# Seven half products for the last four chunks of a squared-ReLU FFN behind a retention layer

## The chip, the core and the metric

One core of a Trainium2 chip runs the whole kernel in one launch. The metric is device time in microseconds (us). Three runs of the kernel before are shown: 203.85, 206.41 and 206.54 us, so the median is 206.41.

The engines are called as in the profile: PE multiplies matrices into the accumulator memory PSUM, DVE and ACT do elementwise work and read PSUM, POOL does elementwise work between buffers in SBUF, SP issues the transfers.

## What is computed

```python
for t in range(S):                       # retention: 4 batches, 8 heads of 64, S = 768
    state = gamma * state + einsum('bhd,bhe->bhde', k[:, :, t], v[:, :, t])
    y[:, :, t] = scale * einsum('bhd,bhde->bhe', q[:, :, t], state)
x = y.transpose(0, 2, 1, 3).reshape(3072, 512)
h = maximum(x @ w_in, 0)                 # first FFN product, 512 -> 2048
out = h * h @ w_out                      # second FFN product, 2048 -> 512
```

Inputs and output are float32; the matrix products read bf16.

## The kernel before, in words

The 3072 rows are 24 chunks of 128 (`C`). For each chunk the kernel loads q, k and v, casts them to bf16 (`ck`, `cq`, `cv`: names that the code gives its operations), transposes k and q (by PE early on, by a transposing transfer `X` later, L753 to L777), and makes a *visit* (`visit`, L828): PE computes scores and state sums of chunk n into the PSUM tensor `sc` and the outputs of chunk m into `yy`. `V22.23` is the visit that finishes chunk 22 and begins 23, `V23.` the one that finishes 23. DVE turns `sc` into the masked scores (`P`, L867) and the new state (`S`, L880), and `yy` into the FFN's input `xt` (`Y`, L889).

The first product (`ffn1`, L917 to L963) goes by blocks, mostly of two chunks. A block has 2048 hidden columns; each operation `F1.b.f` covers two groups of 128 of them with 8 matmuls of 128x256 (L936) into one of four rotating PSUM tensors `fps`. ACT takes the ReLU into a float32 buffer `r` (`R`, L943; there are two such buffers), and ACT (L950) or DVE (L952) squares it into `h` (`Q`). Blocks 11 and 12 are chunks 20 to 23.

The second product of chunks 4 to 23 (`products`, L992 to L1084) is already done with seven products in place of eight for each pair of chunks. DVE makes five sums of parts of `h` (`S1`, `S2`, `S5`, `S6`, `S7`, L1007), PE does seven products `M1` to `M7` of 8 matmuls of 128x256 each (L1032), and DVE and ACT combine them on the way out of PSUM (`e4`, `cc` on ACT, L1054 and L1060; `t1`, `u1`, `w`, `c` on DVE, L1050). SP stores the results.

Operations are declared with what they read and write, and a planner (`Plan`, L19) places all of them before anything is recorded: at each step it takes the operation that can start first by its own assumed durations, with priorities (`prio`, `RANK`, `LAGS`) as tie breaks, `HOME` fixing the engine where several could do the work. It also picks the `fps` tensor. The order it finds is the program's order on each engine. On PE the end of that order is: the visits to `V23.` with blocks 10 and 11 and the products of chunks 14 and 16 between them, then block 12 among the products of 16 to 20, and last `M5.22 M2.22 M7.22 M6.22`.

Of the kernel before, what the change touches and what calls it, by code (L numbers as in the profile page):

```python
# [18 lines left out]
class Plan:  # L19
# [21 lines left out]
    def add(self, name, eng, dur, reads=(), writes=(), fn=None, prio=0.0, lat=0.0, bank=None, after=(), count=0, slot=None, lock=()):  # L41
# [24 lines left out]
        return i

    def schedule(self, nbanks, max_open, nslots):
# [33 lines left out]
        while done < n:  # L102
            best = None
            for eng, cand in pool.items():
                ef = eng_free[eng]
# [22 lines left out]
            (t, _, _), i, eng = best
            o = ops[i]
            for e in o["eng"]:  # L130
                pool[e].discard(i)
# [34 lines left out]
            else:  # L166
                if eng == "PE":
# [21 lines left out]
                    if any(before < x <= issued for x in range(self.BLOCK0 - self.AHEAD, issued + 1, self.BLOCK)):  # L189
# [66 lines left out]
CAST = {"k": {"DVE": 0.43, "ACT": 0.63, "POOL": 0.64}, "q": {"DVE": 0.43, "ACT": 0.63, "POOL": 0.64}}
WCAST = {"DVE": 0.43, "ACT": 0.63, "POOL": 0.64}
EVAC = {"ACT": 0.6, "DVE": 0.62}
WPRIO = {"in": -2.0, "out": 2.0, "sum": 3.0}
# [3 lines left out]
SQUARE = {"DVE": 0.7, "ACT": 0.63}  # L263
WSUM = {"DVE": 0.69}
ASUM = {"DVE": 0.69}
LAGS = {
    16: 4.0, 4: 10.75, 6: 18.25, 10: 2.25, 20: 1.75, 14: 3.0, 8: 2.25, 18: 3.0, 12: 1.75, 22: 2.0,
}
RELU = {"ACT": 0.6}
# [4 lines left out]
PAIRS_A = {"S1": ((0, 0), (1, 1), ALU.add, None), "S5": ((0, 0), (0, 1), ALU.add, None),  # L274
           "S2": ((1, 0), (1, 1), ALU.add, None), "S6": ((1, 0), (0, 0), ALU.subtract, (1, 0)),
           "S7": ((0, 1), (1, 1), ALU.subtract, (0, 1))}
HOME = {
# [930 lines left out]
```

## Time and profile before

| | |
|---|---|
| runs of the kernel before | 203.85, 206.41, 206.54 us |
| span of the profiled execution | 202.7 us |
| time of the profiled execution with what lies around the span | not given on its own; the span lies 1.15 us below the lowest run, 3.7 below the median |
| PE busy | 192.8 us, 3032 matmuls |
| DVE, ACT, POOL busy | 150.0, 130.3, 31.3 us |
| granted PE clock | 1.00 throughout |

The page first gives each engine's busy time, then the span in 40 slices (a digit is tenths of the slice that the engine was busy), then the chain of work that ended last, then groups of equal instructions. A duration in the groups runs from an instruction's start to its modelled end; instructions of one engine overlap at their ends, so the distance between starts is shorter: 8 matmuls of 128x256 take 0.87 us one behind the other although one alone is shown with 264 to 273 ns, and DVE operations of 0.69 us follow each other every 0.61.

### The profile page before, as it was taken

What the parts mean: (1) busy time and instruction counts of PE and PEld (TensorE: products, weight loads), DVE (VectorE), ACT (ScalarE), POOL (GpSimd) and SP (SyncE); (2) the same over time, 40 slices, a digit from 0 to 9 for tenths busy, and PEclk for the clock granted to TensorE, in tenths of its full rate; (3) what the DMA queues carried; (4) which work ended last, traced back from release to release, by engine and by line L of the source; (5) the groups of instructions that cost most, each with busy time, mean ns of one, the idle gap of its engine ahead of it and who ended that gap; (6) DMA issues with size and microseconds to landing.
All of it is one profiled execution on the core that took longest, in us unless ns stands there. A gap on an engine that the chain in (4) does not pass through costs nothing.

```text
span 202.7 us, 7020 instructions
## 1 busy us (share of the span) xinstructions
PE 192.8 (95%) x3032; PEld 159.4 (79%) x3032; DVE 150.0 (74%) x283; ACT 130.3 (64%) x229; POOL 31.3 (15%) x56
## 2 busy tenths in 40 slices
PE   8886999899989999999999999999999999999992
PEld 6554887664577888888888888888888888888881
DVE  3486449569849988969898888878998784934762
ACT  8565888788871883787975485569375873835210
POOL 6541252220102101310211012203010000000000
PEclk9999999999999999999999999999999999999999
DMA  5999999999999999999999999999676100111313
GB/s 159 290 314 320 348 344 330 361 246 210 236 191 219 231 247 212 205 234 186 148 240 165 261 211 218 178 222 194 143 145 97 48 17 3 52 52 55 102 55 105
DMA packets 97935, 38.46 MB, mean 190 GB/s; under 512 B 81008, under 2 KB 94320, under 8 KB 97904
## 3 DMA queue, kind: packets, MB, share of 16 engines
q1 hardware_dynamic: 97760, 37.89, 86.2%
q8 instruction: 23, 0.38, 0.8%
q10 hardware_dynamic: 144, 0.13, 0.2%
q14 instruction: 8, 0.07, 0.1%
HBM read 27.26 MB, written 6.29 MB: 166 GB/s over the span
## 4 chain that ended last, share of the span: by engine, by line
PE 75%; DMA 15%; SPq 5%; POOL 1%; DVE 1%; issue 1%; ACT 0%; DVEq 0%
PE fps L936 33%; PE fps L1032 29%; DMA kn<-in_k_dram 8%; PE fps L1108 6%; DMA wst<-in_moe_w_in_dram 4%; DMA qkT<-kqs 3%; SPq L910 3%; PE yy L787 2%; SPq L537 2%; PE yy L802 1%; PE sc L813 1%; PE sc L824 1%; POOL w_in L522 1%; DVE wu L1050 1%; POOL h L522 0%
## 5 line engine op out<-in xcount | busy, mean ns | idle before, releaser
L936 PE MATMUL fps<-xt,w_in 128*128 128x256 bf16 (+1 forms) x832 | 94.0, 264 | 1.6 <-ACT w_in L518 1.2
L936 PEld LDWEIGHTS <-w_in 128*128 128x128 bf16 x832 | 74.8, 98 | 11.5 <-ACT w_in L518 2.0
L943 ACT ACTIVATE r<-fps 128x512 f32<-128x512 f32 x96 | 56.4, 592 | 34.6 <-PE fps L936 28.6
L950 ACT ACTIVATE h<-r 128x512 bf16<-128x512 f32 x63 | 39.1, 627 | 1.4
L1032 PE MATMUL fps<-wst,h 128*128 128x256 bf16 x320 | 39.4, 273 | 0.0
L1032 PEld LDWEIGHTS <-h 128*128 128x128 bf16 x320 | 31.0, 98 | 3.9
L952 DVE TENSOR_TENSOR h<-r 128x512 bf16<-128x512 f32 x33 | 22.8, 705 | 8.7 <-ACT r L943 8.6
L1032 PEld LDWEIGHTS <-wst 128*128 128x128 bf16 x240 | 23.3, 98 | 2.8
L1007 DVE TENSOR_TENSOR wst<-h 128x1024 bf16<-128x1024 bf16 x30 | 19.4, 685 | 2.9 <-ACT h L950 2.6
L1032 PE MATMUL fps<-w_out,wst 128*128 128x256 bf16 x160 | 20.3, 273 | 0.0
L728 DVE TENSOR_TENSOR vs<-vn,vf 128x512 bf16<-128x512 f32 x20 | 13.8, 691 | 6.3 <-DMA vn<-in_v_dram 6.3
L889 DVE TENSOR_TENSOR xt<-yy,yf 128x512 bf16<-128x512 f32 x20 | 13.7, 687 | 3.5 <-PE yy L802 3.4
L522 POOL CAST kqs<-kn 128x512 bf16<-128x512 f32 x12 | 8.0, 666 | 51.0 <-DMA kn<-in_k_dram 32.3
L1108 PE MATMUL fps<-w_out,h 128*128 128x512 bf16 x64 | 15.0, 379 | 0.7 <-DVE w_out L520 0.7
L1007 DVE TENSOR_TENSOR h<-h 128x1024 bf16<-128x1024 bf16 x20 | 14.0, 729 | 0.2
L880 DVE TENSOR_TENSOR state<-sc,state 128x256 bf16<-128x256 f32 x33 | 13.8, 418 | 0.5
L867 DVE TENSOR_TENSOR pt<-sc,cmask 128x512 bf16<-128x512 f32 x20 | 13.6, 681 | 0.0
L522 POOL CAST kqs<-qn 128x512 bf16<-128x512 f32 x11 | 6.9, 626 | 42.9 <-DMA qn<-in_q_dram 30.6
L1050 DVE TENSOR_TENSOR wu<-fps,wu 128x512 f32<-128x512 f32 (+1 forms) x16 | 9.1, 572 | 5.0 <-ACT osb L1060 2.8
L1108 PEld LDWEIGHTS <-h 128*128 128x128 bf16 x64 | 5.9, 98 | 6.8 <-issue 0.8
L1060 ACT ACTIVATE osb<-fps 128x512 f32<-128x512 f32 x10 | 5.9, 594 | 8.3 <-PE fps L1032 8.3
L1050 DVE TENSOR_TENSOR osb<-fps,osb 128x512 f32<-128x512 f32 (+1 forms) x15 | 9.0, 601 | 2.6 <-PE fps L1032 1.7
(85 smaller groups left out, 173.4 us busy)
## 6 DMA issues: line engine op xcount, KB each, us to landing
qn<-in_q_dram SPq DMA_DIRECT2D x20, 256.0 KB, 5.1
kn<-in_k_dram SPq DMA_DIRECT2D x20, 256.0 KB, 5.6
vn<-in_v_dram SPq DMA_DIRECT2D x20, 256.0 KB, 5.2
out_dram<-osb SPq DMA_DIRECT2D x19, 256.0 KB, 3.3
wst<-in_moe_w_out_dram SPq DMA_DIRECT2D x4, 1024.0 KB, 10.1
wst<-in_moe_w_in_dram SPq DMA_DIRECT2D x4, 512.0 KB, 8.4
wst<-in_moe_w_in_dram SPq DMA_DIRECT2D x2, 1024.0 KB, 8.3
kn<-in_k_dram SPq DMA_DIRECT2D x2, 512.0 KB, 4.3
```

Source lines behind the costliest of these rows:

```text
L522: nc.gpsimd.tensor_copy(o, t)
L728: lambda: nc.vector.tensor_tensor(out=o[:], in0=t.rearrange("s (h d) -> s h d", h=H), in1=vf[:, i, :, None].to_broadcast([P, H, D]), op=AL ...
L880: f = lambda cc=cc, j1=j1, j0=j0: nc.vector.tensor_tensor(out=sts[j1][:], in0=cc, in1=sts[j0][:], op=ALU.add)
L889: lambda: nc.vector.tensor_tensor(out=xt[:, :, u * C : u * C + C].rearrange("s p (g t) -> s g p t", g=2), in0=yy[:, :, 0:256].rearrange("s ...
L936: nc.tensor.matmul(ps[:, u * n : u * n + n], lhsT=w_in_bf[j][:, cb, c * P : (c + 1) * P], rhs=xt[:, cb, cols], start=(cb == 0), stop=(cb = ...
L943: nc.scalar.activation(o, t, AF.Relu)
L950: nc.scalar.activation(hv, rv, AF.Square)
L952: (nc.vector if on == "DVE" else nc.gpsimd).tensor_tensor(out=hv, in0=rv, in1=rv, op=ALU.mult)
L1007: lambda on, o=a[name], x=a[x], y=a[y], op=op: (nc.vector if on == "DVE" else nc.gpsimd).tensor_tensor(out=o, in0=x, in1=y, op=op), prio=c ...
L1032: nc.tensor.matmul(ps[:, 256 * half : 256 * half + 256], lhsT=a[left][:, f], rhs=right(f), start=(first and f == 0), stop=True, skip_group ...
L1050: return lambda ps: nc.vector.tensor_tensor(out=o, in0=ps[:, lo:hi], in1=y, op=op)
L1108: nc.tensor.matmul(ps[:, 0:w], lhsT=h2[:, fb, u * C : u * C + C], rhs=w_out_bf[j][:, c, ns], start=(fb == 0), stop=(fb == NFB - 1))
```

## The change

Blocks 11 and 12 become one block of four chunks (`BLOCKS` ends in 4), done by a new function `ffn1_four`. With the hidden columns in two halves, the model dimension in two halves and the four chunks in two pairs, its eight half products become seven, in the Winograd form. Each of four steps t handles two groups of 128 hidden columns in either half:

- `WI1` to `WI4`, twice each: sums of parts of `w_in`, 128x1024 bf16, written into the load buffers of chunks 20 to 22 after their casts. Five are on DVE, three (`WI4.1`, `WI3.0`, `WI4.0`) on POOL.
- `TX0` to `TX3`: sums of parts of `xt`, 128x512 bf16, on DVE.
- `G1.t` to `G7.t` on PE: 4 matmuls of 128x256 each. `G1`, `G6`, `G7`, `G4` go on accumulating in one PSUM tensor, `G2` stands in a second, `G5` and `G3` accumulate in a third. The first two are the halves of `sc` for t = 0 and 2 and of `yy` for t = 1 and 3, the third is an `fps`.
- between them the accumulators are read while the chain is still open: `kc11`, `kc12`, `kc22` copy one to float32 buffers (11 on ACT, 1 on DVE), `c11`, `c12`, `c22` on DVE add another to the copy (128x512 float32), and `Qc` squares with ReLU: one operation on DVE (5 of them), or a ReLU in place and a square on ACT (7). The fourth quarter is read from the chain's end as before: `R.t` on ACT, `Q.t` on ACT (3) or DVE (1).

```diff
-BLOCKS = [2, 2, 1, 1, 2, 2, 2, 2, 2, 2, 2, 2, 2]
+BLOCKS = [2, 2, 1, 1, 2, 2, 2, 2, 2, 2, 2, 4]
...
+    def ffn1_four(blk):
...
+        for j in range(2):
+            for y, a, b, op in (("1", (1, 0), (1, 1), ALU.add), ("2", "1", (0, 0), ALU.subtract),
+                                ("3", (0, 0), (1, 0), ALU.subtract), ("4", (0, 1), "2", ALU.subtract)):
...
+        for y, a, b, op in ((0, part(0, 1), part(0, 0), ALU.subtract), (1, part(1, 1), tx[0], ALU.subtract),
+                            (2, part(1, 1), part(0, 1), ALU.subtract), (3, part(1, 0), tx[1], ALU.subtract)):
...
+                    for u in range(2):
+                        for k in range(2):
+                            nc.tensor.matmul(ps[:, 256 * u : 256 * u + 256], lhsT=left[i](2 * t + u, k), rhs=right[i][:, k],
+                                             start=(first and u == 0 and k == 0), stop=True, skip_group_check=True)
...
+                    if on == "ACT":
+                        nc.scalar.activation(x, x, AF.Relu)
+                        nc.scalar.activation(o, x2, AF.Square)
+                    else:
+                        (nc.vector if on == "DVE" else nc.gpsimd).scalar_tensor_tensor(
+                            out=o, in0=x2, scalar=0.0, in1=x2, op0=ALU.max, op1=ALU.mult)
...
+            mult(2, "W", True)
+            mult(1, "U", True)
+            kept("c11", "U")
+            both("c11", "W", bkeys["W"])
+            squared("c11", 0, 0)
+            mult(6, "U", False)
+            kept("c12", "U")
+            o1["op"] = pl.ops[mult(5, "V", True)]
+            kept("c22", "V")
+            mult(7, "U", False)
+            both("c22", "U", bkeys["U"])
+            squared("c22", 1, 1)
+            mult(3, "V", False)
+            both("c12", "V", bkeys["V"], bank=("close", ("V", t)))
+            squared("c12", 0, 1)
+            mult(4, "U", False)
```

The priorities and `HOME` go, and `TURNS` writes the order of every engine out by name. SP's order is the same to the end. PE's is the same up to `M4.14`, DVE's up to the sums of chunk 16, ACT's up to `Q10.2`, POOL's to its end, where the three sums are added. In the rest of the program the sums `S1` to `S7` of `products` are renamed `H1` to `H7`. Three squares of block 10 move from DVE to ACT. The end of the new PE order:

```
M4.14 F1.10.8 F1.10.6 V20.21 F1.10.10 F1.10.4 M1.14 M5.14 M2.14 F1.10.12 V21.22 F1.10.14 M6.14 M3.16 M7.14
V22.23 M4.16 M1.16 G2.0 G1.0 V23. M5.16 M2.16 G2.1 G5.0 G1.1 G6.0 M6.16 G3.0 G7.0 G6.1 G5.1 M7.16 G7.1 G4.0
G5.2 G3.1 G4.1 G2.2 M3.18 G1.2 G2.3 G1.3 G5.3 M4.18 G6.2 M1.18 G6.3 G3.2 G7.2 G3.3 G7.3 M5.18 G4.2 G4.3
M2.18 M6.18 M3.20 M4.20 M7.18 M1.20 M5.20 M2.20 M3.22 M4.22 M6.20 M7.20 M1.22 M5.22 M2.22 M7.22 M6.22
```

The planner's assumed durations change too; they move which of the four `fps` an operation gets, and three of the 36 filling matmuls of the start.

More of the change, by code (lines that the diff above doesn't have):

```diff
@@ L34 @@
     HOP = 0.15
+    LATE = 55
+    TAIL = {"DVE": 0.08, "ACT": 0.11, "POOL": 0.055}
     def __init__(self):
@@ L39, in __init__, with add @@
         self.readers = {}
-    def add(self, name, eng, dur, reads=(), writes=(), fn=None, prio=0.0, lat=0.0, bank=None, after=(), count=0, slot=None, lock=()):
+    def add(self, name, eng, dur, reads=(), writes=(), fn=None, lat=0.0, bank=None, after=(), count=0, slot=None, lock=()):
         i = len(self.ops)
@@ L84, in schedule, with offer @@
                 pool.setdefault(e, set())
-                if left[o["i"]] == 0:
-                    pool[e].add(o["i"])
+        known = {o["name"]: o["i"] for o in ops}
+        turns = {e: [known[x] for x in TURNS[e].split()] for e in pool}
+        assert sorted(i for x in turns.values() for i in x) == list(range(n))
+        for e, x in turns.items():
+            for i in x:
+                ops[i]["eng"] = {e: ops[i]["eng"][e]}
+        at = dict.fromkeys(pool, 0)
+        def offer():
+            for e, x in turns.items():
+                if at[e] < len(x) and left[x[at[e]]] == 0:
+                    pool[e].add(x[at[e]])
+        offer()
         if "PE" in eng_free:
@@ L188, in schedule @@
                     history.append((issued, t + dur))
-                    if any(before < x <= issued for x in range(self.BLOCK0 - self.AHEAD, issued + 1, self.BLOCK)):
+                    if t < self.LATE and any(before < x <= issued for x in range(self.BLOCK0 - self.AHEAD, issued + 1, self.BLOCK)):
                         behind = [x for x in moves if x[0] > t + 0.4]
@@ L221, in schedule @@
                 same = list(ops[u]["eng"]) == [eng] and not move
-                ready_at[u] = max(ready_at[u], start[i] + dur if same else end[i] + self.HOP)
+                ready_at[u] = max(ready_at[u], (start[i] + dur if eng not in self.TAIL else end[i] + 0.01) if same else end[i] + self.HOP)
                 left[u] -= 1
-                if left[u] == 0:
-                    for e in ops[u]["eng"]:
-                        pool[e].add(u)
+            offer()
         self.start, self.end, self.on = start, end, [o["on"] for o in ops]
@@ L241 @@
 WARMING = 18.4
-PACE = 8
-LEAD = 2
 NPE = 6
@@ L248 @@
 WHALFD = (0.60, 1.47, 33, 0.6)
-CVT = {'DVE': 0.69, 'POOL': 1.07}
-TCAST = {'DVE': 0.43, 'ACT': 0.63, 'POOL': 0.64}
-TEVAC = {'ACT': 0.6, 'DVE': 0.62}
+CVT = {'DVE': 0.602, 'POOL': 1.003}
+TCAST = {'DVE': 0.338, 'ACT': 0.52, 'POOL': 0.558}
+TEVAC = {'ACT': 0.48, 'DVE': 0.5}
 NPAIR = 2
-F2LAG = 3.5
 F2WAIT = 4
 LAST = [256, 128, 128]
[L256 to L259, printed above, removed]
+CAST = {"k": {"DVE": 0.338, "ACT": 0.52, "POOL": 0.558}, "q": {"DVE": 0.338, "ACT": 0.52, "POOL": 0.558}}
+WCAST = {"DVE": 0.338, "ACT": 0.52, "POOL": 0.558}
+EVAC = {"ACT": 0.48, "DVE": 0.341}
 BOTH = ("DVE", "POOL")
[L263 to L269, printed above, removed]
+SQUARE = {"DVE": 0.602, "ACT": 0.52}
+WSUM = {"DVE": 0.602}
+ASUM = {"DVE": 0.602}
+RELU = {"ACT": 0.48}
+FUSED = ()
+KEPT = {"ACT": 0.48, "DVE": 0.602}
+SQUARE2 = {"DVE": 0.602, "ACT": 1.1}
+WSUM2 = {"DVE": 0.602, "POOL": 2.0}
 APART = (22,)
@@ L273 @@
            "T6": ((0, 0), (0, 1), ALU.add), "T7": ((1, 0), (1, 1), ALU.add)}
[L274 to L277, printed above, removed]
[36 rows of a table removed]
-}
-ROUND = []
-RANK = {
[22 rows of a table removed]
-}
-ORDER = (
-    "k0 q0 v0 q2 k2 v2 i0 i1 i2 q4 i3 i4 k4 i5 v4 o0 q5 o1 k5 o2 o3 q6 v5 k6 v6 q7 k7 v7"
-)
-def dma_order(nm):
-    names = {"i": "in", "o": "out"}
-    seq = [(names.get(t[0], t[0]), int(t[1:])) for t in ORDER.split()]
-    return seq + [(x, m) for m in range(nm) for x in "kqv" if (x, m) not in seq]
+PAIRS_A = {"H1": ((0, 0), (1, 1), ALU.add, None), "H5": ((0, 0), (0, 1), ALU.add, None),
+           "H2": ((1, 0), (1, 1), ALU.add, None), "H6": ((1, 0), (0, 0), ALU.subtract, (1, 0)),
+           "H7": ((0, 1), (1, 1), ALU.subtract, (0, 1))}
+TURNS = {
+    "POOL": (
[3 rows of a table added]
+    ),
+    "DVE": (
[15 rows of a table added]
+    ),
+    "ACT": (
[13 rows of a table added]
+    ),
[8 rows of a table added]
+    ),
[16 rows of a table added]
+    ),
+}
 @with_exitstack
@@ L681, in add_up @@
                     nc.vector.tensor_tensor(out=sts[j1][:], in0=cc, in1=sts[j0][:], op=ALU.add)
-            pl.add(f"S{m + c}", {"DVE": 0.42, "ACT": 0.45} if first else "DVE", 0.42, (f"gB{m + c}",) if first else (f"gB{m + c}", f"S{j0}"), (f"S{j1}",), add_up,
-                   prio=urgency(m) - 0.5, bank=("close", ("B", m + c)))
+            pl.add(f"S{m + c}", {"DVE": 0.341, "ACT": 0.28} if first else "DVE", 0.341, (f"gB{m + c}",) if first else (f"gB{m + c}", f"S{j0}"), (f"S{j1}",), add_up, bank=("close", ("B", m + c)))
         for b2 in range(2):
@@ L703, in out_fn @@
                                         in1=f, op=ALU.mult)
-            pl.add(f"Y{m}.{b2}", "DVE", 0.68, banks[b2] + (f"yf{b2}", f"yf{2 + b2}"),
-                   [f"xt{g % NXT}.{u + c}" for c in range(2)], out_fn, prio=urgency(m))
+            pl.add(f"Y{m}.{b2}", "DVE", 0.602, banks[b2] + (f"yf{b2}", f"yf{2 + b2}"),
+                   [f"xt{g % NXT}.{u + c}" for c in range(2)], out_fn)
     def prepare(m):
@@ L812, in scores, with sums @@
                     cs = slice(sub * L, sub * L + L)
-                    nc.tensor.matmul(sc[cs, a, j * L : j * L + L], lhsT=qkT[r, 0, j, cs], rhs=qkT[r, 1, j, cs],
-                                     start=(j == 0), stop=True, skip_group_check=True)
-    def sums(m):
+                    nc.tensor.matmul(sc[cs, a, 256 * x + j * L : 256 * x + j * L + L], lhsT=qkT[r, 0, j, cs], rhs=qkT[r, 1, j, cs],
+                                     start=(j == 0 and x == 0), stop=True, skip_group_check=True)
+    def sums(m, ps=None, first=False):
         ks, vs = bf["k"][m % NBF], bf["v"][m % NBF]
@@ L823, in sums @@
                 for a in range(2):
-                    nc.tensor.matmul(sc[L * a : L * a + L, sub, 256 + j * D : 256 + j * D + D],
-                                     lhsT=ks[r, j, a, :], rhs=vs[r, 4 * a + j, :],
-                                     start=False, stop=True, skip_group_check=True)
+                    o = sc[L * a : L * a + L, sub, 256 + j * D : 256 + j * D + D] if ps is None else ps[sub][L * a : L * a + L, j * D : j * D + D]
+                    nc.tensor.matmul(o, lhsT=ks[r, j, a, :], rhs=vs[r, 4 * a + j, :],
+                                     start=(first and j == 0), stop=True, skip_group_check=True)
     def visit(m, n, t=None):
@@ L858, in visit @@
             dur += 0.2
-        pl.add(f"V{'' if m is None else m}.{'' if n is None else n}", "PE", dur, reads, writes, fn,
-               prio=-300 + n if m is None else -300 + m if m < PACE else (m - LEAD) * 8, lat=0.25,
+        pl.add(f"V{'' if m is None else m}.{'' if n is None else n}", "PE", dur, reads, writes, fn, lat=0.25,
                count=32 * ((m is not None) + (n is not None) + (t is not None)) + 1)
@@ L881, in visit @@
                         out=sts[j1][:], in0=cc, in1=sts[j0][:], op=ALU.add)
-                pl.add(f"S{n}.{sub}", "DVE", 0.42, (f"sc{sub}",) if first else (f"sc{sub}", f"S{j0}"), (f"S{j1}",), f,
-                       prio=urgency(n))
+                pl.add(f"S{n}.{sub}", "DVE", 0.341, (f"sc{sub}",) if first else (f"sc{sub}", f"S{j0}"), (f"S{j1}",), f)
         if m is not None:
@@ L887, in visit @@
             xt = xts[g % NXT]
-            pl.add(f"Y{m}", "DVE", 0.68, ("yy0", "yy1") + tuple(f"yf{p}" for p in range(NJ)), (f"xt{g % NXT}.{u}",),
+            i0 = pl.add(f"Y{m}", "DVE", 0.602, ("yy0", "yy1") + tuple(f"yf{p}" for p in range(NJ)), (f"xt{g % NXT}.{u}",),
                    lambda: nc.vector.tensor_tensor(
@@ L891, in visit, with visit2, fn, f @@
                        in0=yy[:, :, 0:256].rearrange("s g (p t) -> s g p t", p=NJ),
-                       in1=yf[:, :, i * C : i * C + C].rearrange("s p (g t) -> s g p t", g=2), op=ALU.mult),
-                   prio=urgency(m))
+                       in1=yf[:, :, i * C : i * C + C].rearrange("s p (g t) -> s g p t", g=2), op=ALU.mult))
+            y_made.append(i0)
+    def visit2(ms, ns):
+        reads, writes = [], []
+        for m in ms:
+            reads += [f"bfv{m % NBF}", f"pt{m % 2}"] + qkeys(m) + [f"S{state(m, 0)}", f"S{state(m, 1)}"]
+        if ms:
+            writes += ["yy0", "yy1"]
+        for n in ns:
+            reads += [f"bfk{n % NBF}", f"bfv{n % NBF}"] + qkeys(n)
+        o1 = {}
+        if ns:
+            writes += ["sc0", "sc1", f"gB{ns[0]}.0", f"gB{ns[0]}.1"]
+        def fn():
+            for x, m in enumerate(ms):
+                values(m, x)
+                apply(m, 0, x)
+            if ms:
+                nc.tensor.drain(fusable=True).then_inc(turn, 1)
+                turns[0] += 1
+            for x, n in enumerate(ns):
+                scores(n, x)
+            for x, n in enumerate(ns):
+                sums(n, [fps[o1[sub]["bank_index"]][:, 256 * x : 256 * x + 256] for sub in range(2)], x == 0)
+            if ms:
+                nc.tensor.wait_ge(turn, turns[0])
+                for x, m in enumerate(ms):
+                    apply(m, 1, x)
+        name = ".".join("-".join(str(x) for x in y) for y in (ms, ns))
+        if ns:
+            i0 = pl.add(f"U{name}", "PE", 0.0, reads, writes, lambda: None,
+                        bank=("open", ("U", ns[0], 0), False))
+            o1[0] = pl.ops[i0]
+        i0 = pl.add(f"V{name}", "PE", 0.2 + 0.26 * (len(ms) + len(ns)) + (0.2 if not ns else 0), reads, writes, fn, lat=0.25, count=32 * (len(ms) + len(ns)) + 1,
+                    bank=("open", ("U", ns[0], 1), False) if ns else None)
+        if ns:
+            o1[1] = pl.ops[i0]
+        for x, n in enumerate(ns):
+            pt = pts[n % 2]
+            pl.add(f"P{n}", "DVE", 0.602, ("sc0", "sc1", "cmask"), (f"pt{n % 2}",),
+                   lambda pt=pt, x=x: nc.vector.tensor_tensor(
+                       out=pt[:], in0=sc[:, :, 256 * x : 256 * x + 256].rearrange("s g (p t) -> s g p t", p=NJ),
+                       in1=cmask[:, None, None, :].to_broadcast([P, 2, NJ, L]), op=ALU.mult))
+            for sub in range(2):
+                if sub == 1 and where(n)[1] == NCH - 1:
+                    continue
+                j0, j1 = state(n, sub), state(n, sub + 1)
+                first = where(n)[1] == 0 and sub == 0
+                def f(j0=j0, j1=j1, first=first, sub=sub, x=x):
+                    cc = fps[o1[sub]["bank_index"]][:, 256 * x : 256 * x + 256].rearrange("s (p t) -> s p t", p=NJ)
+                    if first:
+                        nc.vector.tensor_copy(sts[j1][:], cc)
+                    else:
+                        nc.vector.tensor_tensor(out=sts[j1][:], in0=cc, in1=sts[j0][:], op=ALU.add)
+                users = 1 + (sub == 0 or all(where(y)[1] != NCH - 1 for y in ns))
+                pl.add(f"S{n}.{sub}", "DVE", 0.341, [f"gB{ns[0]}.{sub}"] + ([] if first else [f"S{j0}"]), (f"S{j1}",), f, bank=("close", ("U", ns[0], sub), users))
+        for x, m in enumerate(ms):
+            g, u = divmod(m, 4)
+            i = where(m)[1]
+            xt = xts[g % NXT]
+            pl.add(f"Y{m}", "DVE", 0.602, ("yy0", "yy1") + tuple(f"yf{p}" for p in range(NJ)), (f"xt{g % NXT}.{u}",),
+                   lambda xt=xt, u=u, i=i, x=x: nc.vector.tensor_tensor(
+                       out=xt[:, :, u * C : u * C + C].rearrange("s p (g t) -> s g p t", g=2),
+                       in0=yy[:, :, 256 * x : 256 * x + 256].rearrange("s g (p t) -> s g p t", p=NJ),
+                       in1=yf[:, :, i * C : i * C + C].rearrange("s p (g t) -> s g p t", g=2), op=ALU.mult))
@@ L945, in relu, with relu_square @@
                     nc.vector.tensor_scalar_max(o, t, 0.0)
+            def relu_square(f0=f0, o1=o1):
+                t = fps[o1["op"]["bank_index"]][:].rearrange("p (u n) -> p u n", u=per)
+                nc.vector.scalar_tensor_tensor(out=h2[:, f0 : f0 + per, cols], in0=t, scalar=0.0, in1=t,
+                                               op0=ALU.max, op1=ALU.mult)
             def square(on, f0=f0, o1=o1):
@@ L952, in square @@
                     (nc.vector if on == "DVE" else nc.gpsimd).tensor_tensor(out=hv, in0=rv, in1=rv, op=ALU.mult)
-            i0 = pl.add(f"F1.{blk}.{f0}", "PE", per * NCB * (n * 0.4167 + 3) / 1e3, reads, (f"g{grp}",), mm,
-                        prio=blk0[blk] * 8 + 2 * f0 * nb / 4, lat=0.2, bank=("open", grp, False),
-                        count=per * NCB)
+            hk = [f"h{g % NH2}.{u0 + w}.{f0 + u}" for u in range(per) for w in range(nb)]
+            i0 = pl.add(f"F1.{blk}.{f0}", "PE", per * NCB * (n * 0.4167 + (3 if n > C else 10)) / 1e3, reads, (f"g{grp}",), mm, lat=0.2, bank=("open", grp, False),
+                        count=per * NCB, after=openers.get(g - NH2, ()))
@@ L957, in ffn1 @@
+            f1_of.setdefault(g, []).append(i0)
             o1["op"] = pl.ops[i0]
-            hk = [f"h{g % NH2}.{u0 + w}.{f0 + u}" for u in range(per) for w in range(nb)]
-            i0 = pl.add(f"R{blk}.{f0}", RELU, 0, (f"g{grp}",), (f"r{grp}",), relu,
-                        prio=blk0[blk] + f0 / 16 * nb, bank=("close", grp), slot=("open", grp))
+            if f"{blk}.{f0}" in FUSED:
+                pl.add(f"RQ{blk}.{f0}", "DVE", 0.602, (f"g{grp}",), hk, relu_square,
+                       bank=("close", grp), after=twin_users if g == NH2 - 1 else pt_users if g == 1 else ())
+                continue
@@ L1033, in mm @@
                                      start=(first and f == 0), stop=True, skip_group_check=True)
-            k = pl.add(f"M{i}.{c0}", "PE", 0.877, key[left] + reads, (f"gS{c0}{bank}",), mm,
-                       prio=(c0 + 1 + LAGS.get(c0, F2LAG)) * 8 + count[0] * 16 / 7, lat=0.2,
+            k = pl.add(f"M{i}.{c0}", "PE", 0.877, key[left] + reads, (f"gS{c0}{bank}",), mm, lat=0.2,
                        bank=(bank_use, ("s", c0, bank), True) if bank_use == "open" else (bank_use, ("s", c0, bank)), count=8)
@@ L1038, in product, with read @@
             if first:
+                both_open.append(k)
+                openers.setdefault(g, []).append(k)
+            if first:
                 op["op"] = pl.ops[k]
-        def read(name, eng, dur, bank, reads, writes, fn, close=False, prio=0.0):
+        def read(name, eng, dur, bank, reads, writes, fn, close=False):
             pl.add(f"{name}.{c0}", eng, dur, [f"gS{c0}{bank}"] + list(reads), writes,
-                   lambda: fn(fps[opened[bank]["op"]["bank_index"]]), prio=c0 + 1 + prio,
+                   lambda: fn(fps[opened[bank]["op"]["bank_index"]]),
                    bank=("close", ("s", c0, bank)) if close else ("use", ("s", c0, bank)))
@@ L1069, in products @@
             product(7, "B", 0, "use")
[L1070 removed]
+            read("c", "DVE", 0.602, "B", kwu, kwu, on_psum(wu[:], 0, 512, wu[:], ALU.subtract), close=True)
         if last:
@@ L1078, in products @@
                         out[rows(c0) + lo * C : rows(c0) + lo * C + C, col : col + 256], wu[:, 256 * lo : 256 * lo + 256])
-                pl.add(f"st{c0}.{lo}", "ACT" if lo == 0 else "SP", STORE, k, (), f, prio=-1)
+                pl.add(f"st{c0}.{lo}", "ACT" if lo == 0 else "SP", STORE, k, (), f)
             return
@@ L1121, in ffn2 @@
                        lambda q4=q4, slot=slot, ns=ns, at_end=at_end: (nc.scalar if at_end else nc.sync).dma_start(
-                           out[rows(q4) : rows(q4) + C, ns], osbs[slot][:, ns]),
-                       prio=-1)
-    dma_prio = {x: n for n, x in enumerate(dma_order(NM))}
-    urgency = lambda m: m - 3.0
+                           out[rows(q4) : rows(q4) + C, ns], osbs[slot][:, ns]))
     for kind in pieces:
@@ L1141 @@
         n = m + 1
-        for x in range(0 if m < 0 else m + AHEAD, min(NM, m + AHEAD + 1)):
+        if n > DOUBLE:
+            xs = range(prepared, min(NM, n + AHEAD) if n % 2 else prepared)
+        else:
+            xs = range(0 if m < 0 else m + AHEAD, min(NM, m + AHEAD + 1))
+        for x in xs:
             prepare(x)
             transpose(x)
+            prepared = x + 1
         t = m + 2 if NPE <= m + 2 < NTD else None
-        if n < 2 * NPAIR:
+        if n >= DOUBLE:
+            if n % 2 == 0:
+                visit2([x for x in (n - 2, n - 1) if n > DOUBLE or x == n - 1], [x for x in (n, n + 1) if x < NM])
+        elif n < 2 * NPAIR:
             if n % 2 == 0:
@@ L1155 @@
         while done < NB and blk0[done] + blocks[done] - 1 == m:
-            ffn1(done)
+            (ffn1_four if blocks[done] == 4 else ffn1)(done)
             while done2 < NM and done2 + 2 <= blk0[done] and blk0[done] - done2 >= F2WAIT:
```

247 lines of the change are left out of this document (148 added, 99 removed), and 113 rows, old and new, of tables (HOME, RANK, TURNS).

## The prediction

> **What bounds the kernel now.** I read the page first, then the stage that the change touches by its busy times, its chain of waits, its idle PE time, and last some rows that price the new operations.
>
> ```profile
> span 202.7 us, 7020 instructions
> ...
> PE 192.8 (95%) x3032; PEld 159.4 (79%) x3032; DVE 150.0 (74%) x283; ACT 130.3 (64%) x229; POOL 31.3 (15%) x56
> ...
> PE   8886999899989999999999999999999999999992
> ...
> PEclk9999999999999999999999999999999999999999
> ...
> L943 ACT ACTIVATE r<-fps 128x512 f32<-128x512 f32 x96 | 56.4, 592 | 34.6 <-PE fps L936 28.6
> L950 ACT ACTIVATE h<-r 128x512 bf16<-128x512 f32 x63 | 39.1, 627 | 1.4
> ...
> L1007 DVE TENSOR_TENSOR wst<-h 128x1024 bf16<-128x1024 bf16 x30 | 19.4, 685 | 2.9 <-ACT h L950 2.6
> ...
> L880 DVE TENSOR_TENSOR state<-sc,state 128x256 bf16<-128x256 f32 x33 | 13.8, 418 | 0.5
> ...
> L1060 ACT ACTIVATE osb<-fps 128x512 f32<-128x512 f32 x10 | 5.9, 594 | 8.3 <-PE fps L1032 8.3
> ```
>
> PE is at 9 from about a third of the span to the end, at the full clock. The busy times by stretch begin where the orders part (147.8 is `V20.21`, 160.7 `V22.23`):
>
> ```profile
> 147.80:160.70 12.90, 12.90 (x237) 11.27 (x236) 10.79 (x20) 8.66 (x16) 0.61 (x1) 1.00 0.48 82
> 160.70:166.70 6.00, 6.00 (x109) 5.22 (x108) 5.23 (x10) 4.88 (x8) 0.00 (x0) 1.00 0.14 46
> 166.70:175.20 8.50, 8.42 (x106) 7.46 (x105) 5.36 (x10) 4.56 (x9) 0.00 (x0) 1.00 0.01 2
> 175.20:188.40 13.20, 13.20 (x123) 11.84 (x121) 5.89 (x11) 6.56 (x12) 0.00 (x0) 1.00 0.19 61
> 188.40:197.20 8.80, 8.80 (x83) 7.88 (x81) 6.87 (x12) 0.98 (x2) 0.00 (x0) 1.00 0.27 90
> ```
>
> Columns are PE, weight loads, DVE, ACT, POOL, clock, DMA share, GB/s. PE waits for nothing there (0.08 goes around a visit); DVE is busy 34.1 of 49.4 us, ACT 25.6, POOL 0.6. What PE's work ends with:
>
> ```profile
> 186.72 0.87 PE fps L936 x8
> 187.59 9.62 PE fps L1032 x88
> 197.21 0.02 issue
> 197.23 0.61 ACT osb L1060
> 197.84 0.02 issue
> 197.86 0.70 DVE wu L1050
> ```
>
> So a matmul of 128x256 costs 9.62 / 88 = 0.109 us, and 5.5 us of tail follow `M2.22`. The end moves as PE moves.
>
> **The change, part by part.**
>
> *PE.* Blocks 11 and 12 were 2 x 64 matmuls of 128x256; the seven products are 4 steps x 7 x 4 = 112 of the same shape, type and count of columns. 16 x 0.109 = 1.75 us go, all on the path. The visits and the products `M` are the same in number; a change of row size around a visit costs the next group 0.11 (0.98 where 0.87 is usual), as often as before.
>
> *Up to `V20.21`.* Orders are equal; other `fps` numbers put other waits on PE (`M3.12` now waits for `w.10`, say). Held against the trace, each new releaser had ended before the PE operation began, and the three filling matmuls stand where PE waits for a cast: 0.
>
> *ACT.* 25 operations go (16 ReLU, 9 squares), 35 come (11 copies, 4 ReLU, 3 `Q`, 14 for seven `Qc`, 3 squares from DVE). Ten at 0.6 us are 6 us more, 31.6 of 47.6: room on average.
>
> *DVE.* Ten squares of 0.69 go. In come 5 `WI` at 0.685 (L1007), 12 adds, 1 copy, 5 `Qc` and 1 `Q` at 0.69 (the L1050 rows of 512), and 4 `TX`. `TX` is 128x512 bf16: half of L1007's 0.685 is 0.34, a float32 row is 0.69; I take 0.42, L880's for 256 cycles' worth of work, nearest to the half. `Qc` in one operation of two steps has no row: 0.69 if a pass, 1.25 if two (0.6 + 0.63, as ACT's two); I take 0.69, since it reads and writes as L952 does. Together 3.4 + 13.1 + 1.7 - 6.9 = 11.3 us more: 45.4 of 47.6 by durations, but each overlaps its neighbour by 0.08, so about 38 of 47.6. DVE has little room, and what decides is when its results come.
>
> *The new waits.* Each step has PE wait for ACT or DVE to read the open accumulator, with all behind it on PE held. I laid out the tightest place, counting from the end of `V23.` on PE. PE: `M5.16`, `M2.16`, `G2.1` (0.87, 0.87, 0.44), so `G5.0` at 2.2, `G6.0` 3.1, `G7.0` 4.8, `G6.1` 5.2, `G4.1` 8.7. DVE has 3.2 us of work between `c.14` and `Y23` (`P23`, `S23.0`, `Y22`, `t1.16`, two sums) in the 3.3 that PE gives it, then from 0.2: `Y23` 0.61, `u1.16` 0.34, `TX0` done at 1.55 (needed 2.2), `c11.0`, `TX1` done at 2.5 (needed 3.1), `H5.18`, `TX2`, `w.16`, `c11.1` done at 4.7 (needed 5.2). ACT: `G6.0` ends at 3.7, `kc11.1` ends at 3.85, `kc12.0` at 4.45 (needed 4.8). Later ones the same way: 0.35 to 0.6 us of room at each of `G7.1`, `G4.1`, `G2.2`, `G6.2`, `G6.3`, `G7.2`, `G7.3`, over 1 us from `M6.18` on. PE loses nothing with the values taken. With `TX` at 0.69 it loses 0.1 at `G6.0`, 0.25 at `G6.1`, 0.1 at `G4.1`: 0.45. With `Qc` on DVE at 1.25 it loses about 0.9, most at `G6.2` behind three of them. With both, 1.9. Below nothing is excluded: PE has no wait left there to give back.
>
> *Transfers.* SP's order stands. `V22.23` comes 1.2 us earlier than before and needs chunk 23's transpose, issued at 153.1 and landed 3.3 later, 3 us ahead. `t1.22` waits for the store of `c.18`, 2.2 us to landing, with 4 us between: 0.
>
> *POOL.* Its three sums, nearest row L553, 128x512 in 1.04, so 2.1 each for 1024 (bounds 1.04 and 4.2), begin after DVE's `WI2.1`, some 9.1 us ahead of the end of `V23.`, and are needed at `G3.0`, 13.5 us later. But POOL and DVE hold each other up in this trace:
>
> ```profile
> 31.03 1.29 DVE L952 TENSOR_TENSOR h<-r 128x512 bf16<-128x512 f32 x2
> ...
> 34.07 1.69 DVE L952 TENSOR_TENSOR h<-r 128x512 bf16<-128x512 f32 x2
> ```
>
> ```profile
> 9.74 1.04 POOL L553 TENSOR_TENSOR h<-vn,vf 128x512 bf16<-128x512 f32 x1
> ...
> 33.25 1.36 POOL L522 CAST w_out<-wst 128x512 bf16<-128x512 f32 x2 [3.04 <-DMA wst<-in_moe_w_out_dram]
> ```
>
> The same two squares take 1.69 in place of 1.29 while POOL casts. Here `cv23` comes first and holds POOL 0.6; the sums then run from -8.5 to -2.2. DVE's next operation with two SBUF inputs is `H1.18` at -1.2: 1 us clear, 0. The Trainium skill ("SBUF — State Buffer", section "Who interferes with whom") says that a DVE instruction with two SBUF inputs and a GpSimd one that reads SBUF exclude each other for the whole instruction, the first to issue winning; the 1.69 agrees. By that rule the sum is the same unless POOL is slower than the row, and it speaks against the change then. The skill's "GPSIMD Engine Reference" (section 3.1) has an add of 2048 float32 at 4497 ns, by which I estimate 2.25 per sum, still clear.
>
> **Sum.** 202.7 - 1.75 + 0 = 200.95 us of span. The runs stand at two levels, 1.15 and 3.7 above the span; the median moves along: 206.41 - 1.75 = 204.7.
>
> **The rivals.**
>
> *Just in time turns into late.* A duration of 0.7 in place of 0.6 in a chain with 0.35 to 0.6 of room costs some tenths at several `G`; the bounds above give 0.45 to 1.9, I take 0.9. Span 201.85, time 205.6. For it: DVE is laid out with almost no idle time from `P23` to `G4.3`. Against: the margins are of rows measured under the same load.
>
> *Slower: POOL holds DVE.* If its sums last longer than 2.45 each they reach `H1.18`, from 2.6 on `TX0` is late for `G5.0`, at 3.2 the stall eats the 1.75, and at the bound of 4.2 they end at +4.1, `H1.18` is 5.3 late and PE stands about 4.8: 202.7 - 1.75 + 4.8 = 205.75, time 209.5, 1.5% slower. For it: the DVE square stretched by 0.4. Against: L553 is 1.04 three times out of three.
>
> *The same work.* That fewer products don't shorten PE's work is excluded by the count and by a pitch that depends on the shape alone (0.87 for 8, in L936 and L1032 both).
>
> **How the numbers follow.** Forecast 0.65, late 0.24, POOL 0.08, something else 0.03. A measurement of this kernel tells about 2% (4.1 us) from no change, and no mechanism here is that large; a gain over 2% would need the after runs to settle on the lower level (203.85 - 1.75 = 202.1), which I give 0.11. Faster 0.11, within 2% 0.86, slower 0.03. The range reaches from that level, 201.9, over the late case, to the gain all lost, 206.5; for the forecast alone, 202.1 to 205.0.
>
> **What would show it.** 3016 matmuls; PE busy near 191; no idle PE time before `G5.0`, `G6.0`, `G7.0`, `G6.1`, `G6.2`; `TX` near 0.42, `Qc` near 0.69, POOL's sums near 2.1 and over before `H1.18`. PE idle ahead of a `G` with DVE as releaser makes the second case; a stretched `H1.18` or `H6.16` beside POOL the third. I am wrong altogether if PE up to 147.8 differs by more than a few tenths, or the tail after `M2.22` is not 5.5.

## The result and the profile after

The changed kernel takes 202.09 us (median of 22 runs, 201.62 to 204.82), the kernel before 203.91 (22 runs, 203.42 to 206.54). The ratio is 0.9915, with a 95% interval of 0.9904 to 0.9926: 1.7 us faster, of 1.75 forecast. The two of the first three runs near 206.5 turned out to be exceptions, so the median of before lies 2.5 us lower than the one that the forecast started from.

From the page of the changed kernel, the lines that answer to those shown of before (in section 5: busy us, mean ns of one, idle time before and its releaser):

```profile
span 200.5 us, 7020 instructions
...
PE 191.8 (96%) x3011; PEld 158.8 (79%) x3016; DVE 159.4 (79%) x301; ACT 134.8 (67%) x239; POOL 38.1 (19%) x59
...
PE   8987999899999999999999999999999999999993
...
PEclk9996999999999999999999999999999999999999
...
L986 ACT ACTIVATE r<-fps 128x512 f32<-128x512 f32 x80 | 47.1, 593 | 25.9 <-PE fps L979 19.8
...
L1166 DVE TENSOR_TENSOR wst<-h 128x1024 bf16<-128x1024 bf16 x30 | 19.4, 686 | 0.7 <-ACT h L998 0.4
...
L858 DVE TENSOR_TENSOR state<-sc,state 128x256 bf16<-128x256 f32 x33 | 13.8, 419 | 0.4
...
L1221 ACT ACTIVATE osb<-fps 128x512 f32<-128x512 f32 x10 | 6.0, 596 | 8.6 <-PE fps L1191 8.6
```

3016 weight loads are there, 16 fewer than before, one for each matmul; five matmul records are missing from the trace. PE is as full as it was, DVE, ACT and POOL are fuller by 9.4, 4.5 and 6.8 us. The 6 in the row of the clock is a stretch of 3.4 us at half clock from 17.0 us on, which the trace of before doesn't have; no cost of it is seen at `M4.14`, which starts at 146.82 us before and at 146.86 after. Busy times by stretch (PE, weight loads, DVE, ACT, POOL, clock, DMA share, GB/s):

```profile
147.80:159.80 12.00, 12.00 (x225) 10.32 (x223) 10.42 (x20) 8.95 (x17) 5.55 (x4) 1.00 0.42 89
159.80:166.00 6.20, 6.12 (x134) 5.20 (x133) 5.75 (x12) 1.15 (x3) 1.73 (x1) 1.00 0.14 45
166.00:175.00 9.00, 9.00 (x85) 8.09 (x83) 8.47 (x15) 7.65 (x15) 0.00 (x0) 1.00 0.18 60
175.00:188.00 13.00, 13.00 (x121) 11.65 (x120) 12.35 (x21) 10.53 (x20) 0.00 (x0) 1.00 0.07 22
188.00:195.50 7.50, 7.50 (x71) 6.71 (x70) 6.02 (x12) 1.62 (x4) 0.00 (x0) 1.00 0.31 106
```

PE still waits for nothing (0.08 around a visit), while DVE is busy for over nine tenths of 159.8 to 188 us. The view of who waited for whom has no row for PE behind 147 us. The chain's end:

```profile
184.90 10.60 PE fps L1191 x97
195.50 0.02 issue
195.53 0.61 ACT osb L1221
196.13 0.02 issue
196.16 0.70 DVE wu L1211
```

`cc.22` on ACT, which starts when `M2.22` is done, starts at 195.53 in place of 197.23. The clearest measure is the stage by itself. `M4.14` is the last PE operation with the same ones before it in both kernels, `M2.22` sets the tail. From the start of one to the start of the other is 49.34 us before (146.82 to 196.16) and 47.59 after (146.86 to 194.45): 1.75 us less. From the start of `cc.22` to the span's end is 5.4 us before, 5.0 after, so the spans, 202.7 and 200.5, are 2.2 us apart in this one execution of each.

### The profile page after: what moved, and what is told of

The parts are those of the page before. It is cut to its first block, busy times and chain, and to the rows that moved or that the text cites. A ratio compares the mean times of both kernels' runs of the same rounds, so it can differ in the third digit from the quotient of the medians.

```text
span 200.5 us, 7020 instructions
## 1 busy us (share of the span) xinstructions
PE 191.8 (96%) x3011; PEld 158.8 (79%) x3016; DVE 159.4 (79%) x301; ACT 134.8 (67%) x239; POOL 38.1 (19%) x59
## 4 chain that ended last, share of the span: by engine, by line
PE 65%; DMA 22%; SPq 6%; POOL 2%; issue 1%; ACT 1%; DVE 1%; DVEq 0%; POOLq 0%; ACTq 0%
PE fps L1191 27%; PE fps L979 21%; DMA kn<-in_k_dram 8%; DMA qkT<-kqs 7%; PE fps L1269 6%; DMA wst<-in_moe_w_in_dram 4%; DMA qn<-in_q_dram 4%; SPq L954 3%; PE yy L1064 2%; PE sc L1064 2%; SPq L536 2%; PE fps L1064 2%; PE yy L767 2%; PE sc L793 1%; PE yy L782 1%
## 5 line engine op out<-in xcount | busy, mean ns | idle before, releaser
L979 PE MATMUL fps<-xt,w_in 128*128 128x256 bf16 (+1 forms) x704 | 79.0, 266 | 0.9 <-ACT w_in L517 0.9
L979 PEld LDWEIGHTS <-w_in 128*128 128x128 bf16 x704 | 63.1, 99 | 9.4 <-ACT w_in L517 1.5
L986 ACT ACTIVATE r<-fps 128x512 f32<-128x512 f32 x80 | 47.1, 593 | 25.9 <-PE fps L979 19.8
L998 ACT ACTIVATE h<-r 128x512 bf16<-128x512 f32 x57 | 35.3, 628 | 1.1
L711 DVE TENSOR_TENSOR vs<-vn,vf 128x512 bf16<-128x512 f32 x20 | 14.5, 724 | 7.4 <-DMA vn<-in_v_dram 7.4
L1000 DVE TENSOR_TENSOR h<-r 128x512 bf16<-128x512 f32 x23 | 16.2, 721 | 2.7 <-ACT r L986 2.7
L1269 PE MATMUL fps<-w_out,h 128*128 128x512 bf16 x59 | 14.4, 379 | 1.0 <-DVE w_out L519 0.6
L866 DVE TENSOR_TENSOR xt<-yy,yf 128x512 bf16<-128x512 f32 x19 | 13.1, 687 | 2.1 <-PE yy L782 1.9
L1191 PE MATMUL fps<-wst,wst 128*128 128x256 bf16 x80 | 10.4, 273 | 0.0
```

The source lines that it names most:

```text
L711: lambda: nc.vector.tensor_tensor(out=o[:], in0=t.rearrange("s (h d) -> s h d", h=H), in1=vf[:, i, :, None].to_broadcast([P, H, D]), op=AL ...
L866: lambda: nc.vector.tensor_tensor(out=xt[:, :, u * C : u * C + C].rearrange("s p (g t) -> s g p t", g=2), in0=yy[:, :, 0:256].rearrange("s ...
L979: nc.tensor.matmul(ps[:, u * n : u * n + n], lhsT=w_in_bf[j][:, cb, c * P : (c + 1) * P], rhs=xt[:, cb, cols], start=(cb == 0), stop=(cb = ...
L986: nc.scalar.activation(o, t, AF.Relu)
L998: nc.scalar.activation(hv, rv, AF.Square)
L1000: (nc.vector if on == "DVE" else nc.gpsimd).tensor_tensor(out=hv, in0=rv, in1=rv, op=ALU.mult)
```

## The experiments

All are edits of the changed kernel. "Stage" is the time from the start of `M4.14` to the start of `M2.22` in the trace, 47.59 without an edit. A gap on PE is the distance between the starts of two matmuls less the usual 0.109; the view of waits counts from a modelled end and shows it shorter or not at all.

| kernel | stage, us | ratio to before, 95% interval | PE waits |
|---|---|---|---|
| the change | 47.59 | 0.9915 (0.9904 to 0.9926) | none |
| e1_g2_twice | 49.34 | 0.9982 (0.9966 to 0.9997) | none |
| e2_tx0_four | 48.45 | 0.9951 (0.9932 to 0.9969) | `G5.0`, `G6.0` |
| e3_pool_more | 52.18 | 1.009 (1.0059 to 1.0121) | `G2.1`, `G5.0` |
| e4_half_sum | 45.19 | 0.9778 (0.9759 to 0.9797) | ten of the `G` |
| e5_tx0_two | 47.64 | 0.9888 (0.9862 to 0.9915) | none |
| e6_kc11_twice | 47.91 | one run | `G7.0` |
| e7_sums_on_dve | 48.19 | 0.9929 (0.9909 to 0.995) | `M6.14` |

**The 16 matmuls put back.**

```diff
-                    for u in range(2):
-                        for k in range(2):
+                    for _ in range(2 if i == 2 else 1):
+                        for u in range(2):
+                            for k in range(2):
...
```

> The changed kernel with each G2.t done twice (the second start overwrites the first): 16 matmuls of 128x256 more, so that PE has as much to do as before the change, in the new order. Theory (the gain is PE's work): 16 x 0.109 = 1.75 us come back and the ratio to the kernel before is 1.000, within 0.002. Rival (the gain is the new order of the rows around the visits, or the shorter tail): the ratio stays between 0.991 and 0.996.

The stage is 49.34 us, to the hundredth that of the kernel before, with a quite different order of rows. The rival, that the order gained something, falls in the stage. The ratio, 0.9982, is lower than forecast by 0.4 us, with 1.0 just outside its interval; this is not in the stage, and its cause stays open (the tail, in the next section, is one candidate).

**A delay beyond the margin, and one within it.** `TX0` done four times, then twice:

```diff
-                   lambda on, y=y, a=a, b=b, op=op: (nc.vector if on == "DVE" else nc.gpsimd).tensor_tensor(
-                       out=tx[y], in0=a, in1=b, op=op), lock=BOTH, after=f1_of.get(g - 2, ()))
+                   lambda on, y=y, a=a, b=b, op=op: [(nc.vector if on == "DVE" else nc.gpsimd).tensor_tensor(
+                       out=tx[y], in0=a, in1=b, op=op) for _ in range(4 if y == 0 else 1)], lock=BOTH, after=f1_of.get(g - 2, ()))
```

> The changed kernel with TX0 done four times over: three more DVE operations, 1.0 us, in the chain Y23, u1.16, TX0 that G5.0 waits for. In the changed kernel's trace TX0 ends 0.7 us before G5.0 starts. Theory (margins as laid out, and only the part beyond the margin counts): PE waits about 0.4 at G5.0 and in all 0.5, ratio 0.994. Rivals: DVE's place in the chain adds in full, 1.0 us, ratio 0.9965; or PE has other work to go on with, 0, ratio 0.9915.

> The changed kernel with TX0 done twice: 0.34 us more in the chain to G5.0, inside the 0.7 us that the changed kernel's trace leaves. Theory (a delay below the margin costs nothing): from the start of M4.14 to the start of M2.22 147.6 us as without it, no PE wait at G5.0, ratio 0.9915. Rival (DVE's delays add up along the whole stage): 147.9, ratio 0.993.

The lengths of the stage in this expectation and in those of e6 and e7 are written 100 us too high: 147.6 stands for 47.6.

The unedited kernel on DVE, the chain that `G5.0` waits for, and `G5.0`:

```profile
164.00 0.69 DVE L935 TENSOR_TENSOR xt<-yy,yf 128x512 bf16<-128x512 f32 x1 [0.29 <-PE yy L782]
164.61 0.41 DVE L1211 TENSOR_TENSOR osb<-fps,osb 128x256 f32<-128x256 f32 x1
164.94 0.41 DVE L1039 TENSOR_TENSOR xt<-xt 128x512 bf16<-128x512 bf16 x1
166.07 0.60 PE L1064 MATMUL fps<-xt,kn 128*128 128x256 bf16 x4
```

With `TX0` four times:

```profile
163.79 0.69 DVE L935 TENSOR_TENSOR xt<-yy,yf 128x512 bf16<-128x512 f32 x1 [0.29 <-PE yy L782]
164.40 0.42 DVE L1211 TENSOR_TENSOR osb<-fps,osb 128x256 f32<-128x256 f32 x1
164.73 1.79 DVE L1039 TENSOR_TENSOR xt<-xt 128x512 bf16<-128x512 bf16 x4
166.57 0.60 PE L1064 MATMUL fps<-xt,kn 128*128 128x256 bf16 x4 [0.55 <-DVE xt L1039]
```

`TX0` now ends at 166.52, 1.79 after its start in place of 0.41: the delay is 1.38 and not 1.0, since each repetition starts only behind the end of the one before it, which writes the same place (0.46 apart). Less the margin of 0.72 that leaves 0.66, and PE's gap ahead of `G5.0` is 0.71, with 0.16 more at `G6.0`: 0.87 in all, the stage's 48.45 - 47.59 = 0.86. Twice costs 0.05 at most, within what the stage measures. So only what passes the margin counts. The size was off because of the repetitions, not of the margin; the ratio of the second (0.9888) is below the change's own, which nothing in its stage explains.

**The smallest room, on ACT.**

```diff
-                       lambda on, o=c[name]: copy_on(on, o, get()), after=y_made,
+                       lambda on, o=c[name]: [copy_on(on, o, get()) for _ in range(2 if name == "c11" and t == 1 else 1)], after=y_made,
```

> The changed kernel with the copy kc11.1 done twice on ACT, just ahead of kc12.0, which G7.0 waits for: 0.5 us more. In the changed kernel's trace kc12.0 ends 0.4 us before G7.0 starts, the smallest room of all. Theory: PE waits 0.2 us at G7.0 and nowhere else; M4.14 to M2.22 147.8 us. Rival (ACT has room, since it idles between): 147.6, no wait.

The stage grows by 0.32, with a PE gap of 0.27 at `G7.0` and none at other `G`: the place that the theory named, 0.1 us more than it said.

**POOL beside DVE's sums.**

```diff
-                       lambda on, o=wt[y + str(j)], ops_=ops_, op=op: (nc.vector if on == "DVE" else nc.gpsimd).tensor_tensor(
-                           out=o, in0=ops_[0], in1=ops_[1], op=op), lock=BOTH)
+                       lambda on, o=wt[y + str(j)], ops_=ops_, op=op, n=3 if y + str(j) == "40" else 0: (
+                           (nc.vector if on == "DVE" else nc.gpsimd).tensor_tensor(out=o, in0=ops_[0], in1=ops_[1], op=op),
+                           [nc.gpsimd.tensor_tensor(out=room("v", 2), in0=ws(0, 0, 0), in1=ws(1, 0, 0), op=ALU.add)
+                            for _ in range(n)]), lock=BOTH)
```

> The changed kernel with three more sums of 128x1024 bf16 on POOL behind WI4.0, into a load buffer that nobody reads afterwards: POOL goes on from about 161.5 to 167.9 while DVE does H1.18, H6.16 and the chain to TX0 and TX1. Theory (POOL and a DVE operation with two SBUF inputs exclude each other for a whole instruction): H1.18 at 162.4 waits for the end of a POOL sum, 1.2 us, H6.16 perhaps for another, 2.1, and PE stands 0.6 to 4 us at G5.0 and G6.0: ratio 0.995 to 1.011. Rival (they share, and the squares at 34 us were stretched by something else): DVE's times as before, no wait on PE, ratio 0.9915.

POOL in the trace of this kernel, the three sums that are needed and the three added:

```profile
154.35 2.44 POOL L1033 TENSOR_TENSOR qn<-w_in,qn 128x1024 bf16<-128x1024 bf16 x1 [4.81 <-DVE qn L1033]
156.75 2.13 POOL L1033 TENSOR_TENSOR vn<-w_in,w_in 128x1024 bf16<-128x1024 bf16 x1
158.84 2.13 POOL L1033 TENSOR_TENSOR kn<-w_in,qn 128x1024 bf16<-128x1024 bf16 x1
160.92 7.18 POOL L1034 TENSOR_TENSOR vn<-w_in,w_in 128x1024 bf16<-128x1024 bf16 x3
```

DVE beside the added ones (`H1.18`, `H6.16`, `Y23`, `u1.16`, `TX0`, `c11.0`):

```profile
161.86 1.73 DVE L1168 TENSOR_TENSOR wst<-h 128x1024 bf16<-128x1024 bf16 x1
163.51 2.61 DVE L1168 TENSOR_TENSOR h<-h 128x1024 bf16<-128x1024 bf16 x1
166.04 0.68 DVE L935 TENSOR_TENSOR xt<-yy,yf 128x512 bf16<-128x512 f32 x1
166.64 0.41 DVE L1213 TENSOR_TENSOR osb<-fps,osb 128x256 f32<-128x256 f32 x1
166.97 1.41 DVE L1041 TENSOR_TENSOR xt<-xt 128x512 bf16<-128x512 bf16 x1
168.31 0.68 DVE L1081 TENSOR_TENSOR yf<-sc,yf 128x512 f32<-128x512 f32 x1
```

And who waited for whom on PE (total, times, longest):

```profile
PE yy L1066 <- DVE xt L935: 1.5, 1, 1.5
PE fps L1066 <- DVE xt L1041: 1.1, 1, 1.1
```

The three operations that read two SBUF buffers take 1.73, 2.61 and 1.41 where they take 0.69, 0.69 and 0.41 alone. The two between them, with one input in PSUM, take what they always do, with POOL at work all the while. The three added sums, one row above, end at 163.04, 165.57 and 168.10, and each of the three DVE rows ends 0.3 to 0.6 us behind one of these ends. So the exclusion is real, it goes by what DVE reads, and it holds for a whole instruction. The Trainium skill ("SBUF — State Buffer", section "Who interferes with whom") says that a DVE instruction with two SBUF inputs contends with a GpSimd one that reads SBUF, and that the one that comes second is blocked until the first has finished. The 1.73, 2.61 and 1.41 agree. It shows as a longer duration of the DVE row, not as idle time.

PE's first gap is at `G2.1`, which the expectation did not name: it writes into `yy`, which `Y23` has to read first. `TX0` ends 3.59 us later than without the edit, counted from `M4.14`; less the margin of 0.72 that is 2.87, and the two gaps are 1.71 and 1.23, 2.93 in all.

The stage grows by 4.59, though. The other 1.66 is the clock. From 168.81 to 172.22, right behind the second gap, the granted clock in this trace is 0.50, and 16 matmuls follow each other 0.213 us apart. `M6.16`, the 8 matmuls behind `G6.0`, in the unedited kernel and here:

```profile
167.38 1.04 PE L1191 MATMUL fps<-wst,h 128*128 128x256 bf16 x8
...
170.62 1.82 PE L1193 MATMUL fps<-wst,h 128*128 128x256 bf16 x8
```

In the stages of the other traces, where no gap is over 1.15, the clock stays at 1.00. That the gaps brought the half clock on is likely, but no run shows it by itself. The profiled execution took 206.33 us where the median of this kernel is 205.16, so its stage isn't that of every execution: the ratio grows by 0.0175, or 3.6 us, and not by 4.6. At 1.009 the kernel is slower than before.

**The sums on DVE instead.** In `TURNS`, from the end of POOL's list to DVE's:

```diff
-        "ck13 cq13 cq14 ck15 cq15 ck16 ck17 cq18 cq19 ck20 cq20 ck21 cq21 ck22 cq22 ck23 WI4.1 WI3.0 WI4.0 "
+        "ck13 cq13 cq14 ck15 cq15 ck16 ck17 cq18 cq19 ck20 cq20 ck21 cq21 ck22 cq22 ck23 "
...
-        "Q9.12 cv22 Q9.14 H1.16 H5.16 WI1.0 H7.16 WI3.1 WI2.0 t1.14 S21.0 S21.1 H2.16 Y20 WI1.1 P21 WI2.1 cv23 "
+        "Q9.12 cv22 Q9.14 H1.16 H5.16 WI1.0 H7.16 WI3.1 WI2.0 t1.14 S21.0 S21.1 H2.16 Y20 WI1.1 P21 WI2.1 WI4.1 WI3.0 WI4.0 cv23 "
```

> The changed kernel with the three sums WI4.1, WI3.0, WI4.0 on DVE behind WI2.1, none on POOL: 1.8 us more on DVE there, no exclusion by POOL. Theory (DVE has 1.6 us of idle time at c.14, but u1.14, which M6.14 waits for, comes before it): u1.14 ends 0.4 us after M6.14's place, PE waits about 0.5 there, the idle time takes the rest, M4.14 to M2.22 148.1, ratio 0.994. Rival (POOL's part of the work matters only on average, DVE has room): 147.6, ratio 0.9915.

The stage is 48.19, 0.6 us more, and PE's only new gap is 0.61 at `M6.14`, behind `u1.14`. DVE's idle time ahead of `c.14`, 1.60 us before the edit, is 0.22 with it. The ratio's interval holds the expected 0.994 and the rival's 0.9915 both; the trace decides for the theory.

**How near the next bound is.** Here half of each sum over the model dimension is left out:

```diff
-                        for k in range(2):
+                        for k in range(1):
```

> The changed kernel with half of the sum over the model dimension left out in every G (one of two weight parts): 56 matmuls of 128x256 fewer, everything else as it is. Theory (the margins of 0.35 to 0.7 us are all that DVE and ACT have, so PE soon waits for them): of 56 x 0.109 = 6.1 us only some 2 are gained, with PE idle at G6.1, G4.1, G6.2, G7.2 and others, DVE or ACT as releaser: ratio about 0.982. Rival (PE alone sets the end): all 6.1, ratio 0.962.

The rows of PE's waits:

```profile
PE yy L1064 <- DVE yf L1079: 1.2, 2, 1.0
PE sc L1064 <- DVE yf L1079: 0.5, 1, 0.5
PE sc L1064 <- ACT yf L517: 0.3, 1, 0.3
```

Of 6.1 us of matmuls the stage gains 47.59 - 45.19 = 2.4; the runs give 0.9915 - 0.9778 = 0.0137, or 2.8 us, within 0.5. By the starts of its matmuls PE stands about 3.7 us in ten gaps, the longest 1.15 at `G4.1`, 0.67 at `G6.2`, 0.45 at `G7.2`. The view lists four of them, three of these behind DVE's adds. The rival falls. A cut of PE's work in this stage is paid for in full only up to the margins.

## Why the prediction was right

- *PE, 16 x 0.109.* Right to the hundredth: 1.75 in the stage, and 1.75 when the matmuls come back.
- *Up to `V20.21`, 0.* `M4.14` starts at 146.82 and 146.86. Executions scatter more than that: in the kernels above, all with this order, it starts between 145.83 and 146.65.
- *The operations without a row.* By groups of the changed kernel's stage:

```profile
L1091 DVE SCALAR_TENSOR_TENSOR h<-yf 128x512 bf16<-128x512 f32 x5 | 3.3, 683 | 0.0
...
L1088 ACT ACTIVATE yf<-yf 128x512 f32<-128x512 f32 x7 | 4.4, 630 | 0.0
...
L1032 POOL TENSOR_TENSOR vn<-w_in,w_in 128x1024 bf16<-128x1024 bf16 x1 | 2.1, 2127 | 0.0
...
L1039 DVE TENSOR_TENSOR xt<-xt 128x512 bf16<-128x512 bf16 x2 | 0.8, 418 | 0.0
```

  `Qc` on DVE is one pass, 0.683 (0.69 taken, 1.25 the other bound); `TX` 0.418 (0.42 taken); POOL's sum 2.13 (2.1 from the row of half the size).
- *The margins.* `TX0` ended 0.72 ahead of `G5.0` (0.65 laid out), `TX1` 0.66 ahead of `G6.0` (0.6), `c11.1` 0.61 ahead of `G6.1` (0.5), `kc12.0` 0.41 ahead of `G7.0` (0.35). The experiments on `TX0` and `kc11.1` show that these are the margins that count.
- *The load of DVE and ACT.* By the table of stretches DVE was busy for 43.0 of 47.7 us, where about 38 were laid out, and ACT for 29.9, where 31.6 were. The working for DVE took the overlap of 0.08 off all its operations, but the 34.1 us that it started from is a busy time, in which overlaps are counted once. Taken off the 18 added ones alone it gives 44. The mistake had no effect on the forecast, which goes by the margins and not by the sum.
- *POOL.* Its sums ended at 161.53 and `H1.18` began at 162.42: 0.9 clear, 1 forecast. `cv23` held the first for 0.3, not 0.6. The third case was a real danger, as e3 shows, which the placing avoided.
- *What was off: the tail.* The prediction counted 5.5 us behind `M2.22` and called itself wrong altogether if that changed. It did: from `cc.22` to the span's end it is 5.43 us in the one trace of before, and 5.0 in those of the change and of all seven edits. ACT's issue of its half of the last store begins 1.88 us behind `cc.22` in before and after, but takes 0.69 us before and 0.37 after, as in all edits:

```profile
199.11 0.69 ACTq L1077 DMA_DIRECT2D out_dram<-wu  x1
...
197.41 0.37 ACTq L1238 DMA_DIRECT2D out_dram<-wu  x1
```

  Why is open. The DMA view from 195 us on has a transfer of kind "instruction" in before and none in after; that it delays the issue is not shown. With 0.43 us for the tail added to the stages, the ratios of e1, e2, e4, e5 and e7 would be 0.9979, 0.9935, 0.9775, 0.9896 and 0.9923, each inside its interval, and without it e1 and e5 fall just outside. For the change itself it is the other way: 0.9893 with the tail, outside its interval, and 0.9914 without. So 0.4 us of the change's time stay open. The stage, which shows the 1.75 by itself, does not depend on this.
- *What was off: the time.* 204.7 was forecast and 202.09 measured. The miss of 2.6 comes from the median of 206.41 that the forecast started from, for what proved to be 203.91, and not from the change. The time lies inside the range only because its low end allowed for a start from the lowest of the three runs shown; that is owed to the width of the range, not to the mechanism.

## What to carry to other kernels

Where PE never waits, a change is priced by counting its matmuls, and the rest of the work is to show that each new wait is met in time: lay the engines out beside each other from the stage's own rows, and name the margin at each wait. A delay within the margin was free here, and one beyond it cost just the excess in two traces (0.86 and 0.32 us of stage). In a third, gaps of 1.71 and 1.23 us were followed by 3.4 us at half clock, which cost 1.66 more. Room on average (DVE was idle for a tenth of the stage, ACT for over a third) says little. Before work goes to POOL, look at which DVE operations with two SBUF inputs will run beside it.

## What was not expected

One of DVE's sums of weights, `WI3.1`, took 1.10 us in place of 0.69 beside a POOL cast from 148.84 to 149.51; PE shows no wait for it. Repeating a DVE operation into the same place spaces it 0.46 us apart, where different ones of that size follow at 0.34. And the share of a further cut that is earned was only 2.4 of 6.1 us: in this stage, PE-bound for the whole of its length, the margins of DVE's and ACT's work are no more than 0.41 to 0.72 us at the four waits measured.
